# A fused attention and MLP block: DRAM sums sent one per group, a weight combination later in each group, three single window products ahead of the double ones, operand splits in two parts

## The chip, the cores and the metric

The kernel runs on one core of one Trainium2 chip. The metric is the time of one execution in microseconds (us); of several runs the median counts.

## The reference

One input x of 2048 tokens by 576 channels is normalised and goes through two branches, whose sum is the output. Branch A is attention over a dilated window of 8 positions, branch B a token mixer and then an MLP with 4608 hidden channels. All is float32.

```python
def _A_ref(x, wqkv, wo):                      # H = 32 heads of Dh = 18, W = 8, dil = 2
    qkv = (x @ wqkv) -> q, k, v               # by head
    kg, vg = k, v at positions s - 2 * (0..7) # masked before the start
    attn = softmax(einsum("bhsd,bhswd->bhsw", q, kg) * Dh ** -0.5)
    return einsum("bhsw,bhswd->bhsd", attn, vg).reshape(B, S, D) @ wo

def _B_ref(x, w1, w2, w3, w4):
    h = gelu(layernorm(x) @ w1)               # then its quarters shifted by +1, -1, +2, -2 tokens
    x1 = x + shifted(h) @ w2
    return x1 + gelu(layernorm(x1) @ w3) @ w4

xn = layernorm(x)
return x + _A_ref(xn, ...) + _B_ref(xn, ...)
```

## The kernel before

**Numbers and engines.** A float32 value is split into a high part of reduced precision (float32r) and a low part, the rest; a product is made of three matmuls (high by high, high by low, low by high). So each operand is first cast on ScalarE (ACT) and then subtracted on VectorE (DVE). TensorE (PE) does the matmuls, GpSimd (POOL) mainly issues DMAs that add into their destination, SyncE (SP) issues plain DMAs.

**Stages.** After the q, k, v projections, the mixer and the second layer norm, the MLP runs in two stages. In the first, hidden channels are done by `units` u = 0 to 23 (6 pairs of channel blocks by 4 token blocks of 512), with the up product, gelu and down product written out. The second stage does the remaining 24 pairs of hidden blocks and token halves as groups q = 0 to 23; groups 0 to 11 serve the first token half, 12 to 23 the second, with the weights in reverse order. Each of these groups is a 2 by 2 block product done with seven products instead of eight: P1 to P7 multiply sums of weight blocks (tiles `w3a`, with A11, A12, A22, and `w3s`, with S1 to S4) with sums of the activations (B11, B21, B22 from `xn`, and T1 to T4, which are made in DRAM tensors `td` by DMAs that add). Results are gathered in Z1 to Z4 (rows of the tile Y), go through gelu into the hidden tiles `c11`, `c12`, `c21`, `c22`, and D0 to D7 are the down products of the group before, by 128 tokens each. `c12`, `c22` and `c21` have one buffer each, `c11` has two. D0 to D3 read `c12` and `c22`; D4 to D7 read `c11` and `c21`.

**The order.** Nothing schedules the code: each engine carries out its instructions in the order in which they are written. In the second stage a string per group orders PE's work, usually `P1 D0 P2 P6 D1 P5 D2 P7 D3 P4 D4 P3 D5 D6 D7`, in group 11 `P1 D0 P2 P6 P5 P7 D1 P4 P3 D2 D3 D4 D5 D6 D7`, in group 12 `D0 D1 P1 D2 P2 P6 D3 P5 P7 D4 P4 P3 D5 D6 D7`. A `plan` hangs further work behind these steps with `at(step, function)`. The functions that matter:

- `load_pair(q)` (L944, L947) loads the raw W3 blocks into the staging tile `w3st`, which has one buffer; `split_a` casts three of them into `w3a` (ACT L960 and L962, DVE L966) and lets POOL add one 48 KB piece (L963), which reads `w3st`; `combine` (DVE L955, four instructions) then makes the sums in place in `w3st`; `split_s` makes `w3s` from them.
- `sums(sb, step)` (L892 on) builds T1 to T4 of token half sb in DRAM: T1 = n0 top + n1 top, T3 = n1 top + n1 bottom, T2 = n1 bottom + T1, T4 = n0 bottom + T2. Each is one plain DMA from SP and one adding DMA from POOL, 576 KB each.
- `get_op` (L915, L917) loads such an operand, `split_op` (ACT L926 to L928, DVE L595) splits it. In group 11 the operands of the second token half replace those of the first in the same tiles.
- `down` evicts a result: for the ten token tiles in `YD` ACT copies it to a staging tile (L867) and POOL adds it to the DRAM tensor `yd` (L868); for others ACT (L870) or, in the groups around 11 and 12, DVE (L873) adds it in place. Two PSUM banks serve the downs in turn, so Dn needs the eviction of D(n-2). For the in-place tiles ACT first copies the old value into the bank (L843).
- `load_xa(t)` adds the input x to `yd[t]` with a DMA from POOL (L880).
- The attention runs on DVE in the background: after each step `bg` issues some 1.5 us of it, less what the step itself costs DVE (`spent`). For each of 8 groups of four heads the window products are formed in `po` (L740, then a reduction, L743), for one window position (1152 elements per partition) or two at once (2304). `po` has two halves; the first half is also where the output of the head group before is gathered (L716, L720) and stored from to DRAM (`od`, L722). Single products use the second half alone.

## Time and profile before

| what | value |
|---|---|
| median of 3 runs | 1299.88 us (1298.46 to 1302.51) |
| the profiled execution | 1301.5 us |
| its span in the profile | 1299.7 us |
| granted clock of TensorE, mean | 0.994 |
| DMA traffic | 222.66 MB, mean 171 GB/s |

The span runs from the first instruction to the last. An engine's busy time says how much it had to do, not whether it was waited for; the idle time behind "[... <-X]" in a row is what the engine waited in front of that instruction, and X is the instruction or transfer that released it. PEld is the loading of the stationary operand, which runs beside the matmuls; its rows show PE's pauses best. A DMA issued by POOL or SP appears once as an instruction of that engine and once as a transfer, whose "us to landing" counts from its issue.

The groups of the second stage start (P1) at 636.31 us for group 1, then 670.35, 698.24, 725.66, 750.09, 774.15, 798.64, 823.49, 852.61 and 876.95 for groups 2 to 10, 901.01 for group 11, 955.16 for group 13.

### The profile page before, as it was taken

To read this page: it belongs to the slowest core of one execution; us is meant where nothing else is said; L and a number is where in the kernel's file an instruction comes from. 1 tells how busy PE (TensorE), PEld (TensorE's weight loads), DVE (VectorE), ACT (ScalarE), POOL (GpSimd) and SP (SyncE) were. 2 spreads that over 40 slices of the span, in tenths; PEclk is the share of its full clock that TensorE was granted. 3 is DMA by queue.
4 is the path that set the end of the run, shared out by engine and by line. 5 is a ranking of instruction groups with operands and counts; after the bars stand their busy time and mean duration, and the time that the engine had idled before them with its cause. 6 is when DMAs were issued, how large, how long until landed. Compare 5 with 4: busy or idle time off the path is not lost.

```text
span 1299.7 us, 19930 instructions
## 1 busy us (share of the span) xinstructions
PE 1266.1 (97%) x7510; PEld 1158.8 (89%) x7510; DVE 897.3 (69%) x1180; ACT 727.7 (56%) x1162; POOL 252.3 (19%) x366
## 2 busy tenths in 40 slices
PE   8999999999999999999898999899899999999998
PEld 8999998898899998999687998898889999998898
DVE  6456535778568999997556988789788993455342
ACT  3322226526645545556656777667867777667730
POOL 2011100021122212111123232222122222222100
PEclk9999999999999999999999999999999999999999
DMA  7646874246898886769479988868956777899972
GB/s 210 155 112 144 172 165 144 71 141 178 201 264 173 183 170 120 195 125 234 82 200 202 191 154 205 169 156 161 281 104 145 157 134 142 189 219 218 255 249 83
DMA packets 203009, 222.66 MB, mean 171 GB/s; under 512 B 79504, under 2 KB 138736, under 8 KB 202784
## 3 DMA queue, kind: packets, MB, share of 16 engines
q1 hardware_dynamic: 170160, 154.59, 41.4%
q0 software_dynamic: 32752, 66.80, 32.7%
q8 instruction: 59, 0.97, 0.3%
q14 instruction: 38, 0.31, 0.1%
HBM read 122.75 MB, written 107.28 MB: 177 GB/s over the span
## 4 chain that ended last, share of the span: by engine, by line
PE 54%; issue 5%; DMA 5%; ACT 4%; DVE 2%; POOL 1%; SPq 1%; POOLq 0%; DVEq 0%; ACTq 0%
PE ps L862 26%; PE cc L1116 15%; PE p L826 10%; PE ps L214 4%; DMA w3a<-w3st 2%; DMA w3st<-in_B_w_dram 1%; POOL yd L868 1%; DMA x1n<-xn 1%; ACT Y L867 1%; DVE w3st L955 0%; DMA xt<-td1T 0%; ACT c L814 0%; ACT w3s L962 0%; DMA yd<-Y 0%; DVE po L720 0%
## 5 line engine op out<-in xcount | busy, mean ns | idle before, releaser
L862 PEld LDWEIGHTS ps<-w,c 128*128 128x128 f32 x3456 | 478.3, 189 | 36.4 <-ACT Y L867 9.9
L862 PE MATMUL ps<-w,c 128*128 128x288 f32 x3456 | 491.7, 296 | 17.0 <-ACT Y L867 7.6
L868 POOL DMA_DIRECT2D yd<-Y x154 | 140.7, 931 | 450.1 <-ACT Y L867 377.0
L820 DVE TENSOR_TENSOR c<-Y,c 128x512 fp32r<-128x512 f32 x144 | 98.9, 687 | 90.5 <-ACT Y L809 78.8
L867 ACT COPY Y<-ps 128x576 f32<-128x576 f32 x154 | 97.8, 636 | 80.7 <-PE ps L862 66.9
L214 PE MATMUL ps<-WQ,xt 128*128 128x432 f32 x672 | 134.8, 360 | 0.0
L1116 PE MATMUL cc<-xt,w3s 128*128 128x512 f32 (+1 forms) x504 | 129.4, 397 | 3.4 <-DVE Y L1126 3.4
L214 PEld LDWEIGHTS ps<-WQ,xt 128*128 128x128 f32 x672 | 125.6, 188 | 5.7
L1116 PEld LDWEIGHTS cc<-xt,w3s 128*128 128x128 f32 (+1 forms) x504 | 93.2, 190 | 21.7 <-DVE Y L1126 3.6
L1116 PE MATMUL cc<-x1n,w3a 128*128 128x512 f32 (+1 forms) x336 | 87.5, 400 | 3.7 <-ACT cc L1310 1.8
L740 DVE TENSOR_TENSOR po<-q,k 128x2304 f32<-128x2304 f32 (+1 forms) x40 | 83.0, 2075 | 7.7 <-DMA od<-po 7.0
L743 DVE TENSOR_REDUCE L<-po 128x128 f32<-128x2304 f32 (+1 forms) x40 | 82.8, 2071 | 0.6
L121 POOL TENSOR_TENSOR rs<-rs,mhalf 128x1 f32<-128x1 f32 x48 | 30.9, 643 | 260.5 <-DVE rs L120 147.9
L323 ACT COPY stg<-ps 128x864 f32<-128x864 f32 x24 | 21.2, 882 | 102.8 <-PE ps L214 55.8
L955 DVE TENSOR_TENSOR w3st<-w3st 128x384 f32<-128x384 f32 x92 | 51.3, 557 | 37.8 <-DMA w3a<-w3st 18.9
L808 ACT ACTIVATE c<-p 128x512 fp32r<-128x512 f32 x48 | 28.7, 599 | 86.8 <-PE p L826 86.8
L716 DVE TENSOR_TENSOR po<-v,L 128x1152 f32<-128x1152 f32 x56 | 75.6, 1354 | 0.9
L1116 PEld LDWEIGHTS cc<-x1n,w3a 128*128 128x128 f32 (+1 forms) x336 | 61.4, 191 | 16.1 <-ACT cc L1310 2.2
L870 ACT COPY Y<-ps 128x576 f32<-128x576 f32 x92 | 58.9, 640 | 30.0 <-PE ps L862 28.5
L720 DVE TENSOR_TENSOR po<-po 128x1152 f32<-128x1152 f32 x49 | 66.4, 1356 | 1.0
L843 ACT COPY ps<-Y 128x576 f32<-128x576 f32 x92 | 59.4, 645 | 3.5 <-DVE Y L873 1.5
L214 PE MATMUL ps<-W,h 128*128 128x288 f32 x384 | 53.5, 295 | 0.0
(194 smaller groups left out, 1935.9 us busy)
## 6 DMA issues: line engine op xcount, KB each, us to landing
yd<-Y POOLq DMA_DIRECT2D x156, 288.0 KB, 6.2
Y<-in_B_w_dram SPq DMA_DIRECT2D x29, 576.0 KB, 7.5
w3st<-in_B_w_dram SPq DMA_DIRECT2D x56, 256.0 KB, 6.2
qkvd<-stg SPq DMA_DIRECT2D x24, 432.0 KB, 3.5
yd<-ev POOLq DMA_DIRECT2D x26, 288.0 KB, 6.5
w3st<-in_B_w_dram SPq DMA_DIRECT2D x92, 64.0 KB, 6.7
xd<-st SPq DMA_DIRECT2D x16, 320.0 KB, 6.0
xd<-big SPq DMA_DIRECT2D x16, 320.0 KB, 8.5
```

Source lines behind the costliest of these rows:

```text
L214: pe.matmul(ps[:, h, :n], xs(a), ws(b, h), start=i == 0, stop=i == len(PAIRS) - 1)
L716: dve.tensor_tensor(dst, vv, Lf[:, :, w:w + 1].to_broadcast([128, TPP * GH, HD]), op=ALU.mult)
L720: dve.tensor_tensor(o, o, dst, op=ALU.add)
L740: dve.tensor_tensor(dst, qf[:, None, :].to_broadcast([128, n, TPP * GC]), win, op=ALU.mult)
L743: dve.tensor_reduce(Lw[:, w:w + n, :], dst.rearrange("p w (x d) -> p w x d", d=HD), axis=AX.X, op=ALU.add)
L820: dve.tensor_tensor(h[:, 1, :], g, h[:, 0, :].bitcast(F32), op=ALU.subtract)
L826: pe.matmul(ps, W3[f][:, w, :], x1n[b][:, a, :], start=n == 0, stop=n == len(PAIRS) - 1)
L843: act.copy(ps[:, :, :HF], halves(t))
L862: pe.matmul(ps[:, k, :HF], h[:, col], w[:, p, k * HF:(k + 1) * HF], start=n == 0 and not seed, stop=n == len(seq) - 1, skip_group_check=True)
L867: act.copy(e.rearrange("p (h c) -> p h c", h=2), ps[:, :, :HF])
L868: pool.dma_start(yd[t], e, accum_op=ALU.add)
L1116: pe.matmul(ps, WX[w][:k, v, SLOT[w], :], area[sb][xk][:k, a, :], start=onto is None and i == 0, stop=last and i == len(HALVES) - 1, skip_ ...
```

## The change

Five things change.

1. `sums` has eight steps with one DMA each instead of four steps with four, two, one and one. In the first stage they are called in units 4 to 11, in the second behind D6 of groups 1 to 8 (before: behind D2 of groups 1 to 4).
2. `load_xa` of groups 1 to 10 goes from P3 to D7.
3. `combine` goes from D3 to P4, in group 0 from D3 to P3 behind the gelu of Z2, in group 12 from D3 to D4.
4. `split_op` can be called in two parts (two of the three thirds of an operand, then the rest). In groups 11 and 12 the parts are spread over more steps, and the gelus, their low parts and `split_w4` of group 11 go to earlier steps.
5. The window products of the attention are three single ones, two double ones and a single one, instead of two single and three double ones.

```diff
-                for w, n in ((0, 1), (1, 1), (2, 2), (4, 2), (6, 2)):
+                for w, n in ((0, 1), (1, 1), (2, 1), (3, 2), (5, 2), (7, 1)):
...
     def sums(sb, step):
         n0, n1 = xn[2 * sb], xn[2 * sb + 1]
-        if step == 0:
-            sp.dma_start(td[sb, "T1"], n1[0:HF])
-            sp.dma_start(td[sb, "T3"], n1[HF:])
-            sp.dma_start(td[sb, "T2"], n1[HF:])
-            sp.dma_start(td[sb, "T4"], n0[HF:])
-        elif step == 1:
-            pool.dma_start(td[sb, "T1"], n0[0:HF], accum_op=ALU.add, max_dma_last_dim=2048)
-            pool.dma_start(td[sb, "T3"], n1[0:HF], accum_op=ALU.add, max_dma_last_dim=2048)
...
+        k, src, first = (("T1", n1[0:HF], True), ("T1", n0[0:HF], False),
+                         ("T3", n1[HF:], True), ("T3", n1[0:HF], False),
+                         ("T2", n1[HF:], True), ("T2", td[sb, "T1"], False),
+                         ("T4", n0[HF:], True), ("T4", td[sb, "T2"], False))[step]
+        if first:
+            sp.dma_start(td[sb, k], src)
...
+            pool.dma_start(td[sb, k], src, accum_op=ALU.add, max_dma_last_dim=2048)
...
+    def split_op(sb, k, part=None):
...
+        if part != 1:
+            spent[0] += 1.2
+            act.activation(xt[:, 3:5, :], raw[:, 1:3, :], AF.Identity, scale=sg)
+        if part != 0:
+            spent[0] += 0.7
+            rtemps.append(rtemps.pop(0))
+            r = temp(rtemps[-1]).bitcast(F32R)
+            act.activation(r[64:96], raw[64:96, 0, :], AF.Identity, scale=sg)
+            act.activation(xt[0:64, 0, :], raw[0:64, 0, :], AF.Identity, scale=sg)
+        if part != 1:
+            signed(xt[:, 1:3, :], raw[:, 1:3, :], sg, xt[:, 3:5, :])
+        if part != 0:
+            signed(xt[64:96, 0, :], raw[64:96, 0, :], sg, r[64:96])
...
-        if 4 <= u < 12 and u % 2 == 0:
-            sums(0, (u - 4) // 2)
+        if 4 <= u < 12:
+            sums(0, u - 4)
...
-            at("D3", combine, n)
             at("P3", gelu12)
-            at("P3", split_s, n, (0, 1))
+            at("P3", combine, n)
             at("P3", low12)
+            at("P3", split_s, n, (0, 1))
             at("P3", split_s, n, (2,))
...
-            at("D1", split_op, 1, "B11")
-            at("D2", split_op, 1, "B21")
-            at("D3", gelu22)
-            at("D4", low22)
-            at("D4", split_op, 1, "T2")
-            at("D5", gelu12)
-            at("D2", split_w4, p)
-            at("D6", low12)
-            at("D6", split_op, 1, "T1")
-            at("D7", split_op, 1, "T4")
+            at("P4", split_w4, p)
+            at("P4", gelu22)
+            at("P3", split_op, 1, "B11", 0)
+            at("P3", low22)
+            at("D2", split_op, 1, "B11", 1)
+            at("D2", gelu12)
+            at("D3", split_op, 1, "B21", 0)
+            at("D4", low12)
+            at("D4", split_op, 1, "B21", 1)
+            at("D5", split_op, 1, "T2", 0)
+            at("D6", split_op, 1, "T2", 1)
+            at("D7", split_op, 1, "T1", 0)
         elif q == NWP:
...
-            at("D1", split_op, 1, "T3")
+            at("D0", split_op, 1, "T1", 1)
+            at("D1", split_op, 1, "T3", 0)
+            at("P1", split_op, 1, "T3", 1)
+            at("D2", split_op, 1, "T4", 0)
             at("P2", split_a, n, (0, 1))
-            at("D2", split_op, 1, "B22")
             at("P6", split_a, n, (2,))
-            at("D3", combine, n)
+            at("P6", split_op, 1, "T4", 1)
+            at("D3", split_op, 1, "B22", 0)
+            at("P5", split_op, 1, "B22", 1)
+            at("D4", combine, n)
...
-            at("D3", combine, n)
             at("D3", split_w4, p, 0)
+            at("P4", combine, n)
...
-        if 0 < q < 5:
-            at("D2", sums, 1, q - 1)
+        if 0 < q < 9:
+            at("D6", sums, 1, q - 1)
         if 0 < q <= len(YD):
-            at("P3", load_xa, YD[q - 1])
+            at("D7", load_xa, YD[q - 1])
```

Three places show how it moves instructions. The first is POOL, from D1 of group 2 to D1 of group 3. td1T1 and the others are the sums (before L900 and L901, now L901), in_A_x is load_xa (L880), yd1 to yd7 are the evictions, w3a and w3s the small pieces of the W3 splits. Before:

```order
L868 DMA yd5_89<-Y_71 128x576 [waits DMASW3_49,Activation_49]
L963 DMA w3a_6258<-w3st_6170 32x384 [waits DMAHW1_49,DMASW4_49,Activation_49]
L900 DMA td1T1_104<-xn2_98 288x512 [waits DMAHW2_49,DMASW5_49]
L901 DMA td1T3_106<-xn3_99 288x512 [waits DMAHW3_49,DMASW6_49]
L868 DMA yd7_90<-Y_71 128x576 [waits Activation_49]
L963 DMA w3s_6360<-w3st_6170 32x512 [waits DVE_49,DMASW0_49,PE_49,Activation_49]
L880 DMA yd2_87<-in_A_x_dram 128x576 [waits DMASW1_49]
L868 DMA yd1_86<-Y_71 128x576 [waits DMASW2_49,Activation_49]
L868 DMA yd2_87<-Y_71 128x576 [waits DMASW3_49,DMASW1_49,Activation_49]
L868 DMA yd3_88<-Y_71 128x576 [waits DMASW4_49,Activation_49]
L868 DMA yd5_89<-Y_71 128x576 [waits DMASW5_49,Activation_49]
L963 DMA w3a_6497<-w3st_6402 32x384 [waits DMAHW3_49,DMASW6_49,Activation_49]
```

Now:

```order
L868 DMA yd5_89<-Y_71 128x576 [waits DMASW3_49,Activation_49]
L964 DMA w3a_6263<-w3st_6173 32x384 [waits DMAHW5_49,DMASW4_49,Activation_49]
L868 DMA yd7_90<-Y_71 128x576 [waits DMASW5_49,Activation_49]
L964 DMA w3s_6358<-w3st_6173 32x512 [waits DVE_49,DMASW6_49,PE_49,Activation_49]
L868 DMA yd1_86<-Y_71 128x576 [waits DMASW2_49,Activation_49]
L868 DMA yd2_87<-Y_71 128x576 [waits DMASW0_49,Activation_49]
L901 DMA td1T1_104<-xn2_98 288x512 [waits DMAHW0_49,DMASW1_49]
L868 DMA yd3_88<-Y_71 128x576 [waits Activation_49]
L880 DMA yd2_87<-in_A_x_dram 128x576 [waits DMASW3_49,DMASW0_49]
L868 DMA yd5_89<-Y_71 128x576 [waits DMASW4_49,Activation_49]
L964 DMA w3a_6502<-w3st_6398 32x384 [waits DMAHW5_49,DMASW5_49,Activation_49]
```

The pair of sums between the w3a piece and yd7 has become one, behind yd2, and load_xa stands behind the three evictions that end the group. In this group it waits for the eviction into its own tensor, yd2, where before the eviction waited for it.

The second place is ACT in group 11, from D1's eviction (L867) on. c22 is cleared for writing by L814 (gelu22), x1n2 is the operand B11 (and B21), w4 the cast of split_w4. Before:

```order
L867 COPY Y_71<-ps1_8276 128x576 [waits DMASW4_49,PE_49]
L926 ACTIVATE x1n2_5540<-x1n2_5540 128x1024 [waits DMAHW3_49]
L927 ACTIVATE Y_71<-x1n2_5540 32x512 [waits DMAHW6_49]
L928 ACTIVATE x1n2_5540<-x1n2_5540 64x512 [waits DMAHW5_49,DMAHW4_49]
L926 ACTIVATE x1n2_5540<-x1n2_5540 128x1024 [waits DMAHW7_49]
L927 ACTIVATE Y_71<-x1n2_5540 32x512 [waits DMAHW2_49,DVE_49]
L928 ACTIVATE x1n2_5540<-x1n2_5540 64x512 [waits DMAHW1_49,DMAHW0_49]
L567 CAST w4_8292<-Y_71 128x2x576
L867 COPY Y_71<-ps1_8382 128x576 [waits DMASW5_49,PE_49]
L814 ACTIVATE c22_8454<-Y_71 128x512 [waits DVE_49]
```

Now:

```order
L867 COPY Y_71<-ps1_8287 128x576 [waits DMASW3_49,PE_49]
L567 CAST w4_8304<-Y_71 128x2x576 [waits DMAHW2_49]
L814 ACTIVATE c22_8410<-Y_71 128x512 [waits DVE_49,PE_49]
L815 ACTIVATE Y_71<-Y_71 128x512 [waits Activation_49]
L921 ACTIVATE x1n2_5548<-x1n2_5548 128x1024 [waits DMAHW3_49]
L926 ACTIVATE Y_71<-x1n2_5548 32x512 [waits DMAHW6_49]
L927 ACTIVATE x1n2_5548<-x1n2_5548 64x512 [waits DMAHW5_49,DMAHW4_49]
L814 ACTIVATE c12_8445<-Y_71 128x512 [waits DVE_49]
L815 ACTIVATE Y_71<-Y_71 128x512 [waits Activation_49]
L867 COPY Y_71<-ps1_8395 128x576 [waits DMASW4_49]
```

The gelu into c22 stands ahead of B11's cast and of D3's eviction (the last row, ps1_8395), and has a wait for PE of its own, which it did not have behind D3's eviction.

The third place is DVE where one head group of the attention ends and the next but one begins, in group 8. L716 and L720 gather the output, L740 is a window product, L743 its reduction, L955 (now L956) the combination. Before:

```order
L716 TENSOR_TENSOR po<-v,L 128x1152 [waits DVE_49]
L820 TENSOR_TENSOR c_7593<-Y,c_7593 128x512 [waits PE_49,Activation_49]
L720 TENSOR_TENSOR po<-po 128x1152 [waits DVE_49]
L740 TENSOR_TENSOR po<-q,k 128x1152 [waits DMAHW1_49,DVE_49]
L743 TENSOR_REDUCE L<-po 128x64 [waits DVE_49]
L740 TENSOR_TENSOR po<-q,k 128x1152 [waits DVE_49]
L743 TENSOR_REDUCE L<-po 128x64 [waits DVE_49]
L820 TENSOR_TENSOR c_7636<-Y,c_7636 128x512 [waits Activation_49]
L740 TENSOR_TENSOR po<-q,k 128x2304 [waits DMAHW0_49,DVE_49]
L966 TENSOR_TENSOR w3a<-w3st,w3a 128x768 [waits DMAHW2_49,DMAHW1_49,Activation_49]
L1126 TENSOR_TENSOR Y<-cc_7661,Y 128x512 [waits Activation_49]
```

Now:

```order
L720 TENSOR_TENSOR po<-po 128x1152 [waits DVE_49]
L740 TENSOR_TENSOR po<-q,k 128x1152 [waits DMAHW0_49,DVE_49]
L743 TENSOR_REDUCE L<-po 128x64 [waits DVE_49]
L740 TENSOR_TENSOR po<-q,k 128x1152 [waits DVE_49]
L820 TENSOR_TENSOR c_7646<-Y,c_7646 128x512 [waits Activation_49]
L743 TENSOR_REDUCE L<-po 128x64 [waits DVE_49]
L967 TENSOR_TENSOR w3a<-w3st,w3a 128x768 [waits DMAHW1_49,DMAHW0_49,Activation_49]
L1127 TENSOR_TENSOR Y<-cc_7671,Y 128x512 [waits Activation_49]
L740 TENSOR_TENSOR po<-q,k 128x1152 [waits DVE_49]
L743 TENSOR_REDUCE L<-po 128x64 [waits DVE_49]
L956 TENSOR_TENSOR w3st<-w3st 128x3x128 [waits DMAHW3_49,DMAHW4_49,DMAHW2_49,DMAHW5_49,DMASW7_49,DMASW1_49]
```

The double product, which waits for the store of the first half of po (DMAHW0), stood ahead of this group's w3a subtraction and its addition to Z3 (L966, L1126). Now these come first, and there are three single products and the combination before it; it follows at the start of group 9.

14 lines of the change are left out of this document (1 added, 13 removed).

## The prediction

> **What bounds the kernel now.** I read the page's totals first, then the second half of the MLP cut into its groups (from one P1 to the next), then the tensor engine's waits, then the engines named there.
>
> ```profile
> span 1299.7 us, 19930 instructions
> PE 1266.1 (97%) x7510; PEld 1158.8 (89%) x7510; DVE 897.3 (69%) x1180; ACT 727.7 (56%) x1162; POOL 252.3 (19%) x366
> ...
> PE   8999999999999999999898999899899999999998
> ```
>
> PE is busy for 97% of the span, and the change leaves its matmuls as they are. Only the 33.6 us in which PE has nothing to do, and the slower matmuls behind its longer pauses, can be won or added to. The table by groups (length, then busy time of each engine, clock, DMA share, GB/s) tells where they lie:
>
> ```profile
> 636.31:670.35 34.04, 26.75 (x145) 23.18 (x146) 14.61 (x21) 19.22 (x31) 6.69 (x8) 0.95 0.55 143
> 670.35:698.24 27.89, 24.76 (x148) 22.16 (x146) 17.38 (x17) 16.29 (x27) 7.92 (x9) 0.99 0.86 193
> 698.24:725.66 27.42, 25.66 (x147) 23.01 (x147) 22.22 (x27) 19.48 (x30) 9.17 (x11) 0.95 0.90 171
> 725.66:750.09 24.43, 24.33 (x148) 21.84 (x147) 22.69 (x25) 18.49 (x31) 7.93 (x10) 1.00 1.05 228
> 774.15:798.64 24.49, 24.32 (x147) 21.96 (x146) 20.06 (x23) 15.15 (x25) 6.24 (x9) 1.00 0.86 203
> 798.64:823.49 24.85, 24.32 (x147) 21.85 (x146) 23.30 (x25) 21.99 (x34) 7.44 (x10) 1.00 0.69 132
> 823.49:852.61 29.12, 25.74 (x148) 23.02 (x146) 21.63 (x22) 15.38 (x25) 6.87 (x9) 0.94 0.79 172
> 901.01:955.16 54.15, 50.57 (x293) 45.40 (x292) 43.84 (x51) 37.87 (x59) 10.49 (x14) 0.97 0.90 214
> 979.21:1003.28 24.07, 24.07 (x148) 21.95 (x147) 21.49 (x26) 17.12 (x28) 5.94 (x8) 1.00 0.75 170
> ```
>
> The last row is a group that waits for nothing: 24.07 us is the floor. Above it stand group 1 (10.0 us), groups 2 and 3 (3.8 and 3.4), groups 4, 6 and 7 (0.4, 0.4 and 0.8), group 8 (5.1), and the pair 11 and 12 (54.15 less 48.14: 6.0). The pauses themselves, in the order of time (start, busy, what, idle before and its releaser):
>
> ```profile
> 643.24 0.98 PEld L862 LDWEIGHTS ps<-w,c 128*128 128x128 f32 x4 [3.54 <-ACT c L814]
> 644.62 1.94 PEld L862 LDWEIGHTS ps<-w,c 128*128 128x128 f32 x8 [0.41 <-DVE c L820]
> 668.79 1.61 PEld L862 LDWEIGHTS ps<-w,c 128*128 128x128 f32 x12 [2.94 <-ACT Y L867]
> 704.86 1.44 PEld L1116 LDWEIGHTS cc<-x1n,w3a 128*128 128x128 f32 x7 [2.00 <-ACT cc L1310]
> 844.83 2.63 PEld L1116 LDWEIGHTS cc<-xt,w3s 128*128 128x128 f32 x7 [3.61 <-DVE Y L1126]
> 921.81 9.49 PEld L862 LDWEIGHTS ps<-w,c 128*128 128x128 f32 x60 [3.08 <-DVE Y L873]
> ```
>
> PE waits for ACT and DVE, which are not full either. So what do they wait for? The groups of DVE's lines, and its rows at three of these places:
>
> ```profile
> L955 DVE TENSOR_TENSOR w3st<-w3st 128x384 f32<-128x384 f32 x92 | 51.3, 557 | 37.8 <-DMA w3a<-w3st 18.9 <-issue 15.2 <-DVE Y L1126 0.9
> 639.58 2.34 DVE L955 TENSOR_TENSOR w3st<-w3st 128x384 f32<-128x384 f32 x4 [2.33 <-DMA w3a<-w3st]
> 641.84 0.68 DVE L1126 TENSOR_TENSOR Y<-cc,Y 128x512 f32<-128x512 f32 x1
> 643.88 0.69 DVE L820 TENSOR_TENSOR c<-Y,c 128x512 fp32r<-128x512 f32 x1 [1.36 <-ACT Y L815]
> 664.13 2.34 DVE L955 TENSOR_TENSOR w3st<-w3st 128x384 f32<-128x384 f32 x4 [6.30 <-DMA w3a<-w3st]
> 840.75 2.56 DVE L740 TENSOR_TENSOR po<-q,k 128x2304 f32<-128x2304 f32 x1 [5.58 <-DMA od<-po]
> ```
>
> The combination (L955) has to wait until the small accumulating DMA of split_a has read the staging tile it overwrites, and the whole of DVE waits with it. At 840.75 it is the attention that holds DVE: a product of two windows writes both halves of po, and one half is still being stored.
>
> ```profile
> td1T<-xn SPq DMA_DIRECT2D x4, 576.0 KB, 7.6
> w3a<-w3st POOLq DMA_DIRECT2D x1, 48.0 KB, 9.5
> 669.15 1.07 POOL L880 DMA_DIRECT2D yd<-in_A_x_dram  x1
> 675.57 2.68 POOL L868 DMA_DIRECT2D yd<-Y  x3 [5.35 <-ACT ps L843]
> 682.50 0.64 ACT L867 COPY Y<-ps 128x576 f32<-128x576 f32 x1 [4.79 <-DMA yd<-Y]
> 695.10 0.91 POOL L901 DMA_DIRECT2D td1T<-xn  x1 [5.82 <-issue]
> 702.47 0.83 POOL L880 DMA_DIRECT2D yd<-in_A_x_dram  x1 [4.70 <-issue]
> ```
>
> The first two rows are the DMA view of 648 to 672 us: the four sums that SP sends at once, and beside them the w3a transfer of 48 KB that needs 9.5 us. Then POOL stands behind load_xa (its yd[1] is accumulated into right behind it, at D5), issues three evictions late, and ACT waits for a staging tile. In group 2 the second of two accumulating sums holds POOL for 5.82 us, and the next load_xa follows 4.70 late.
>
> **The change part by part.** Sums are made against the profiled execution, 1301.5 us (its span of 1299.7 and 1.8 around it), which is 1.6 above the median of the runs, 1299.88.
>
> *Entry into group 1.* In group 0 the combination goes behind the addition to Z2 and its gelu; only the low part still follows it. Before: combination until 641.92, addition at 641.84, gelu, low part at 643.88. Now the low part can start when the combination ends, 641.92: 1.96 earlier, and D0, whose eight matmuls at 644.62 waited for it, moves with it. **-2.0.**
>
> *Group 1.* The four SP sums beside the w3a transfer become one, a group's end away from it. The transfer took 2.33 after DVE was ready in group 0, with nothing beside it, and there is now one attention step and the next matmul stage in front of the combination. The 6.30 falls below the slack, and with it the 2.94 at 668.79. **-3.0.**
>
> *Groups 2 and 3.* load_xa goes from P3 to D7, behind the evictions of the same group. It can still hold POOL while an eviction into its own tile lands (groups 1 to 3 only), but behind it stand just the next group's D1 and its w3a transfer, five stages away (P1, D0, P2, P6, D1: 8 us by the 24.07 over 15 stages). The pair of POOL sums is broken up. The two groups lost 7.2; I leave 2.0 for the loads of q, k and v, which stay. **-5.2.**
>
> *Group 8.* A third single product comes ahead of the first double one. As the order shows, the double now stands behind the rest of the group, not two singles after the store: three singles with their reductions, the combination (2.34), a low part and the w4 split come between, over 10 us against the 5 or so before, and 5.58 was missing. **-4.8** of the 5.1. The price is two more DVE instructions in each of eight head groups. Two halves against one whole:
>
> ```profile
> L716 DVE TENSOR_TENSOR po<-v,L 128x1152 f32<-128x1152 f32 x56 | 75.6, 1354 | 0.9
> 1065.83 1.35 DVE L720 TENSOR_TENSOR q<-q,po 128x1152 f32<-128x1152 f32 x1
> ```
>
> An instruction over 1152 elements takes 1.354 and one over 2304 took 2.56 (840.75), so a split costs 2.71 less 2.56, 0.15, and sixteen cost 2.4 us of DVE. The attention ends at 1067, and it is only forced to end at P4 of group 18, which begins at 1075.5 (979.21 and four more groups of 24.07); without that cover the 2.4 would stand on the path.
>
> *Groups 4 to 10.* Until now these had no sum after group 4; now groups 1 to 8 have one each, sent at D6 with load_pair, whose landing the first step of the next split_a needs by D1. The median landing of load_pair's large pieces was, in the views of 648 to 672 and of 822 to 846:
>
> ```profile
> w3st<-in_B_w_dram SPq DMA_DIRECT2D x2, 256.0 KB, 3.2
> w3st<-in_B_w_dram SPq DMA_DIRECT2D x2, 256.0 KB, 9.3
> ```
>
> 3.2 alone and 9.3 in a crowd, so a sum beside it can cost between nothing and 6.1 of landing; D6 to D1 leaves about 8 to 10. Below nothing is possible too, since the load_xa leaves the stage before. Bounds for the seven groups: they lose the 1.6 they have now less all of it, or as much as group 3 lost with its sum (3.4) in every second one (13). I take **+1.5**, near the low end, since group 4 ran with a sum at a DMA share of 1.05 and lost only 0.4.
>
> *Groups 11 and 12.* Here the splits are cut in two and the gelu of Z3 (gelu22) goes from D3 to P4. But in group 11 P4 comes before D2 and D3, and both still read c22 of the group before, of which there is one buffer. ACT therefore stops at gelu22 until D3 is done, and D4 follows D3 directly. Between them now lie, one after the other: two gelus, the cast of B11, its subtraction on DVE, the low part of c22, and D2's eviction on DVE, which frees D4's bank. Rows of the same instructions:
>
> ```profile
> 914.80 1.06 ACT L926 ACTIVATE x1n<-x1n 128x1024 fp32r<-128x1024 f32 x1 [1.55 <-DMA x1n<-xn]
> 921.15 0.63 ACT L814 ACTIVATE c<-Y 128x512 fp32r<-128x512 f32 x1
> 921.81 0.63 ACT L815 ACTIVATE Y<-Y 128x512 f32<-128x512 f32 x1
> 921.00 0.75 DVE L873 TENSOR_TENSOR Y<-ps,Y 128x576 f32<-128x576 f32 x1
> 921.67 1.22 DVE L595 SCALAR_TENSOR_TENSOR x1n<-x1n 128x1024 fp32r<-128x1024 f32 x1
> ```
>
> 0.63 + 0.63 + 1.06 + 1.22 + 0.69 + 0.75 is 5.0, against the 3.08 that D4 waits today for B11's late landing (914.80). ACT is also busy almost without a break from there on, so a late start is carried along. From 0 (the parts fill gaps of ACT) to +5 (nothing is made up), I take **+2.0**.
>
> The stall of 5.0 is followed by slow matmuls: 2.63 for seven weight loads at 844.83, behind 3.61 idle, 1.44 at 704.86 behind 2.00. The Trainium skill ("TensorE: Matmul & The Clock Gate", Part 1) says that the clock halves after an idle window of about 3.4 us; the trace agrees in so far as 2.94 at 668.79 left full speed behind. By that rule the transition would cost some 1 to 1.5 more, which lies within the +5.
>
> The first half's sums, now one a unit in units 4 to 11, I take at nothing: slices 13 to 18 of PE's row on the page (390 to 585 us), which hold them, stand at nine tenths or more, and the up products there do not wait for them.
>
> Sum: -2.0 - 3.0 - 5.2 - 4.8 + 1.5 + 2.0 = -11.5. 1301.5 - 11.5 = 1290.0 as a profiled execution, less 1.6: **1288.4** for the median.
>
> **The rivals.**
> *Crowding moves to D6.* Load_pair, the sum, three evictions, load_xa and the w4 load now stand within ten us. For it: 9.3 for a load_pair in a crowd. Against it: group 4's 24.43. Each of groups 1 to 8 would lose about 1.2 (a third of the mean of group 2's and 3's loss, 3.6): +9.6 instead of +1.5, 1296.5. The Trainium skill ("DMA: Bandwidth & Descriptors", Queues, rings and completion order) has each DMA engine take turns between queues, packet by packet, which speaks for this one: a sum from POOL would take half the engines' turns from load_pair. No run here shows the turns one by one.
> *Slower: POOL is held at D7.* One mechanism: load_xa at D7 waits for an eviction to land or for room behind a sum, and holds the next w3a transfer; then the combination stops DVE in each of ten groups. The point is a wait on POOL over about 8 us (5.82 is the longest so far). Price: the 8.2 of groups 1 to 3 are not won, and 1.3 in ten groups is lost (a third of the 3.8 in group 2): 1288.4 + 8.2 + 13 = 1309.6.
> *The transition breaks.* ACT, 5 us late at gelu22, never catches up, and T1, T3, T4 and B22 each come late: +8 instead of +2, 1294.4.
> *The double product's order does nothing*, since the store starts elsewhere in a group: 1293.2.
>
> **How the numbers follow.** Forecast 0.58, crowding 0.17, POOL held 0.08, broken transition 0.09, double product 0.08. A measurement here tells 0.3% from nothing, that is 1296.0 to 1303.8. Faster: 0.58 + 0.09 + 0.08 = 0.75. Same: most of crowding, 0.16. Slower: 0.09. The forecast's own bounds are 1281.3 (groups 2 and 3 without the 2.0 left to them, groups 4 to 10 at -1.6 instead of +1.5, +0 in the transition) to 1294.0 (+5 in the transition, half of the 5.2 in groups 2 and 3). Reaching into crowding gives 1281 to 1299.
>
> **What would show it.** Right: no DVE wait over 2 us at the combination in groups 1 to 3; groups 1 to 4 and 8 under 25 us apart from group 1's entry; no wait of ACT for yd; a PE pause of about 5 us ahead of D4 in group 11, with ACT idle at gelu22. Wrong: DVE still waits for w3a, or new pauses at D1 to P4 behind a late load_pair in groups 5 to 8.

## The result, and the profile after

| kernel | median, us | of runs | lowest to highest |
|---|---|---|---|
| before | 1299.22 | 12 | 1297.83 to 1303.91 |
| changed | 1304.09 | 12 | 1301.96 to 1307.86 |

The ratio is 1.0037, 95% interval 1.0024 to 1.0050: slower by 0.4%, where 1288.4 and a gain were forecast. The profiled execution took 1304.09 us.

The page's first lines: the same matmuls, sixteen more DVE instructions, as expected, and a longer span.

```profile
span 1302.3 us, 19944 instructions
PE 1267.3 (97%) x7510; PEld 1162.0 (89%) x7510; DVE 900.6 (69%) x1196; ACT 728.4 (56%) x1162; POOL 252.4 (19%) x366
```

To compare kernels group by group I use the copy of `cc` on ACT, which follows P1 once in every group from 1 on; from one copy to the next lie 24.06 us where nothing waits. The table by stretches, groups 1 to 10 and then 11 and 12 together (length, then busy time of each engine, clock, DMA share, GB/s):

```profile
640.97:665.27 24.30, 24.30 (x141) 22.03 (x140) 10.53 (x14) 16.87 (x29) 6.45 (x8) 0.96 0.53 102
665.27:689.33 24.06, 24.06 (x147) 21.94 (x146) 21.46 (x21) 17.19 (x28) 6.28 (x8) 1.00 0.77 162
689.33:718.42 29.09, 26.13 (x147) 23.16 (x146) 22.99 (x25) 20.16 (x30) 8.73 (x10) 0.94 0.83 197
718.42:742.49 24.07, 24.07 (x147) 21.95 (x146) 20.82 (x22) 17.00 (x28) 5.94 (x7) 1.00 0.97 226
742.49:773.36 30.87, 26.79 (x147) 24.17 (x146) 23.63 (x21) 17.05 (x27) 9.50 (x11) 0.89 0.74 135
773.36:797.83 24.47, 24.32 (x147) 21.96 (x146) 19.58 (x25) 17.00 (x28) 5.23 (x7) 1.00 0.81 211
797.83:825.49 27.66, 25.85 (x147) 23.45 (x146) 22.57 (x23) 20.13 (x30) 8.73 (x11) 0.94 0.77 148
825.49:849.55 24.06, 24.06 (x147) 21.93 (x146) 21.94 (x22) 17.18 (x27) 5.99 (x8) 1.00 0.93 227
849.55:875.25 25.70, 24.31 (x147) 21.96 (x146) 19.88 (x19) 16.99 (x27) 7.88 (x9) 1.00 0.80 147
875.25:901.76 26.51, 24.59 (x147) 22.00 (x146) 22.57 (x27) 19.50 (x29) 7.26 (x9) 1.00 0.77 185
901.76:958.41 56.65, 50.31 (x292) 45.47 (x291) 43.81 (x50) 38.03 (x59) 10.88 (x14) 0.97 0.86 205
```

Groups 1, 2 and 8, which had lost most before, now lose next to nothing. In their place groups 3, 5, 7 and 9 lose: exactly the groups behind a group whose sum is one of POOL's. (Group 10 loses 2.5 as well; experiment 5 shows where that comes from.) What happens in group 3, on POOL (the sum of group 2 at D6, D7's eviction, load_xa at D7, then the evictions of the next group and its w3a transfer):

```profile
690.14 0.94 POOL L901 DMA_DIRECT2D td1T<-xn  x1 [1.83 <-issue]
693.26 0.89 POOL L868 DMA_DIRECT2D yd<-Y  x1 [2.18 <-ACT ps L843]
700.94 0.83 POOL L880 DMA_DIRECT2D yd<-in_A_x_dram  x1 [6.79 <-issue]
701.78 0.90 POOL L868 DMA_DIRECT2D yd<-Y  x1
702.33 1.15 POOL L964 DMA_DIRECT2D w3a<-w3st  x1
```

and on ACT, DVE and PE, in the same order of events:

```profile
697.84 0.62 ACT L963 ACTIVATE w3a<-w3st,kv 96x384 fp32r<-96x384 f32 x1
...
708.70 2.34 DVE L956 TENSOR_TENSOR w3st<-w3st 128x384 f32<-128x384 f32 x4 [3.72 <-DMA yd<-Y]
...
711.11 1.04 ACT L961 CAST w3s<-w3st 128x1024 fp32r<-128x1024 f32 x1 [1.83 <-issue]
...
713.36 1.72 PEld L862 LDWEIGHTS ps<-w,c 128*128 128x128 f32 x12 [2.42 <-ACT Y L867]
```

The first transfer behind the sum goes out 3.1 us after it, the second only 10.8 us after it (in groups 4, 6 and 8 the first after 2.8 to 3.3, the second after 9.6, 10.3 and 9.3). ACT had the w3a piece ready at 698.46 (697.84 and 0.62), and its transfer is issued at 702.33, 3.9 late. By the DMA view of 688 to 706 us it takes 6.3 us, so it lands at 708.6. DVE stands 3.72 at the combination, which starts at 708.70 (the row names the transfer of an eviction issued beside w3a), ACT's cast of w3s waits for it, the eviction L867 stands behind that cast, and PE waits for the bank. The combination's row over the whole kernel, with all that DVE waited there:

```profile
L956 DVE TENSOR_TENSOR w3st<-w3st 128x384 f32<-128x384 f32 x92 | 51.3, 558 | 36.7 <-issue 23.5 <-DMA yd<-Y 3.7 <-DMA xd<-big 2.6
```

36.7 us against 37.8 before: the wait that the change was to remove has only moved.

### The profile page after: what moved, and what is told of

Same layout as the page of the kernel before. It is cut to its first block, busy times and chain, and to the rows that moved or that the text cites. A ratio compares the mean times of both kernels' runs of the same rounds, so it can differ in the third digit from the quotient of the medians.

```text
span 1302.3 us, 19944 instructions
## 1 busy us (share of the span) xinstructions
PE 1267.3 (97%) x7510; PEld 1162.0 (89%) x7510; DVE 900.6 (69%) x1196; ACT 728.4 (56%) x1162; POOL 252.4 (19%) x366
## 5 line engine op out<-in xcount | busy, mean ns | idle before, releaser
L862 PE MATMUL ps<-w,c 128*128 128x288 f32 x3456 | 494.4, 297 | 25.9 <-ACT Y L867 11.9
L867 ACT COPY Y<-ps 128x576 f32<-128x576 f32 x154 | 97.6, 634 | 76.2 <-PE ps L862 71.2
L740 DVE TENSOR_TENSOR po<-q,k 128x1152 f32<-128x1152 f32 (+1 forms) x48 | 84.2, 1754 | 0.8
L743 DVE TENSOR_REDUCE L<-po 128x64 f32<-128x1152 f32 (+1 forms) x48 | 84.0, 1751 | 0.8
L956 DVE TENSOR_TENSOR w3st<-w3st 128x384 f32<-128x384 f32 x92 | 51.3, 558 | 36.7 <-issue 23.5
L716 DVE TENSOR_TENSOR po<-v,L 128x1152 f32<-128x1152 f32 x56 | 75.2, 1354 | 0.9
L720 DVE TENSOR_TENSOR po<-po 128x1152 f32<-128x1152 f32 x49 | 66.4, 1355 | 1.0
```

Of the source, the lines that this page charges most:

```text
L716: dve.tensor_tensor(dst, vv, Lf[:, :, w:w + 1].to_broadcast([128, TPP * GH, HD]), op=ALU.mult)
L720: dve.tensor_tensor(o, o, dst, op=ALU.add)
L740: dve.tensor_tensor(dst, qf[:, None, :].to_broadcast([128, n, TPP * GC]), win, op=ALU.mult)
L743: dve.tensor_reduce(Lw[:, w:w + n, :], dst.rearrange("p w (x d) -> p w x d", d=HD), axis=AX.X, op=ALU.add)
L862: pe.matmul(ps[:, k, :HF], h[:, col], w[:, p, k * HF:(k + 1) * HF], start=n == 0 and not seed, stop=n == len(seq) - 1, skip_group_check=True)
L867: act.copy(e.rearrange("p (h c) -> p h c", h=2), ps[:, :, :HF])
```

## The experiments

Sixteen kernels ran, each against the kernel before on the same chip. In the table, beside median and ratio, what the profile shows: the start of the first copy of `cc` (entry), and what each group lost over 24.06, worked out from the starts of that copy in each kernel's trace. From group 13's copy to the end, a part that most of these edits leave alone, single profiles differ by up to 3.7 us (341.1 to 344.8), so a row of this table is read group by group, and the medians tell what an edit is worth. The kernel before ran again with each set of experiments (medians 1299.22 to 1300.90), so a difference between two kernels can come out up to 1.5 us otherwise by the ratios than by the medians, which the text uses where it does not say ratios.

| kernel | median | ratio, 95% interval | entry | groups 1 to 10 | 11+12 |
|---|---|---|---|---|---|
| before | | | 645.32 | 2.9 7.9 -0.2 -0.1 0 1.3 -0.1 5.5 -0.1 0 | 6.0 |
| changed | 1304.09 | 1.0037 (1.0024 to 1.0050) | 640.97 | 0.2 0 5.0 0 6.8 0.4 3.6 0 1.6 2.5 | 8.5 |
| 1 changed, load_xa at P3 | 1303.29 | 1.0022 (1.0013 to 1.0031) | 643.55 | -0.7 3.6 4.6 0 4.8 0.5 2.6 0 0.2 2.4 | 9.1 |
| 2 changed, sums at D2 | 1293.55 | 0.9948 (0.9933 to 0.9964) | 642.70 | 1.4 0 1.9 2.1 0 0.4 0 0 0 2.3 | 9.3 |
| 3 changed, combination at D3 | 1307.17 | 1.0056 (1.0041 to 1.0071) | 641.09 | 0.3 0 3.5 0 6.3 0.5 5.4 0 3.5 2.2 | 9.5 |
| 4 changed, old plans of 11, 12 | 1303.14 | 1.0026 (1.0011 to 1.0040) | 642.17 | 0.1 0 3.2 0 6.4 0.5 4.7 0 6.3 0 | 5.6 |
| 5 before, third single product | 1296.73 | 0.9976 (0.9964 to 0.9988) | 645.20 | 3.4 3.9 4.7 0 0 0.5 0 0 0 1.6 | 6.1 |
| 6 before, sums singly at D6 | 1305.78 | 1.0044 (1.0021 to 1.0066) | 645.49 | 0 2.5 2.5 -0.1 3.8 1.3 4.2 5.2 2.2 -0.1 | 5.8 |
| 7 before, sums singly at D2 | 1291.95 | 0.9938 (0.9922 to 0.9955) | 644.98 | 1.0 2.6 -0.1 0 0 1.6 -0.1 4.6 -0.1 0 | 5.8 |
| 8 changed, POOL's sums in 8 KB rows | 1302.94 | 1.0017 (0.9995 to 1.0039) | 641.10 | 0.2 0 7.1 0 5.4 0.6 0.2 0.4 6.2 3.5 | 8.8 |
| 9 changed, POOL's sums at D2, SP's at D6 | 1293.68 | 0.9957 (0.9942 to 0.9972) | 643.63 | 0.8 0 2.2 2.8 0 0.5 0 0 1.4 1.7 | 9.5 |
| 10 two parts: 5 and 7 | 1286.95 | 0.9903 (0.9886 to 0.9920) | 644.15 | 0.3 0 1.7 0 0 0.4 0 0 0 1.6 | 5.1 |
| 11 three parts: 10, combination later | 1285.86 | 0.9891 (0.9874 to 0.9908) | 640.97 | 1.6 0 1.7 0 0 0.2 0 0 0 1.3 | 5.3 |
| 12 as 11, load_xa at D7 | 1293.84 | 0.9952 (0.9938 to 0.9967) | 642.42 | 0.9 0 2.4 2.3 0 0.6 0 0 0 2.1 | 7.7 |
| 13 as 11, D7 in groups 1 to 3 | 1288.66 | 0.9907 (0.9888 to 0.9925) | 643.13 | 0.9 0 2.0 2.8 0 0.4 0 0.2 0 1.9 | 6.0 |
| 14 as 11, D7 in groups 4 to 10 | 1288.65 | 0.9905 (0.9884 to 0.9926) | 643.36 | 0.8 0.2 2.0 0 0 0.6 0 0.1 0 1.8 | 7.9 |
| 15 as 11, load_xa in groups 13 to 22 | 1284.34 | 0.9867 (0.9843 to 0.9891) | 642.91 | 0.5 0 0.9 0 0 0.1 0 0 0 0 | 4.5 |
| 16 as 11, POOL's sums in 8 KB rows | 1285.50 | 0.9889 (0.9866 to 0.9911) | 643.70 | 0.9 1.1 2.3 0 0 0.5 0 0 0 1.1 | 6.5 |

**1. load_xa back at P3.**

```diff
-            at("D7", load_xa, YD[q - 1])
+            at("P3", load_xa, YD[q - 1])
```

> The changed kernel with load_xa back at P3; the sums stay at D6, one per group. Theory (POOL is held): with nothing of POOL's behind the sum at D6 but D7's eviction, the waits of 5.6 to 6.8 us on POOL before load_xa (L880) go, the combine of groups 3, 5, 7 and 9 no longer waits 3.7 to 4.3, and the time falls by 4 to 7 us to 1297 to 1300. Rival (crowding: the sum slows load_pair and the w3a transfer on the DMA engines, and POOL's order does not matter): the combine still waits over 3 us in those groups and the time stays within 2 us of 1304.

The gain is 0.8 us (2.0 by the ratios, whose intervals overlap): the theory missed in this form, and the rival's number came. POOL around the sum of group 2, and the combination behind it:

```profile
697.59 0.94 POOL L901 DMA_DIRECT2D td1T<-xn  x1 [0.28 <-issue]
703.54 0.89 POOL L868 DMA_DIRECT2D yd<-Y  x1 [5.01 <-ACT w3a L961]
709.18 0.85 POOL L868 DMA_DIRECT2D yd<-Y  x1 [4.75 <-issue]
709.73 1.12 POOL L964 DMA_DIRECT2D w3a<-w3st  x1
```

```profile
715.08 2.34 DVE L956 TENSOR_TENSOR w3st<-w3st 128x384 f32<-128x384 f32 x4 [4.80 <-DMA w3a<-w3st]
```

Without load_xa it is the next eviction that is held, here until 11.6 us after the sum (9.8, 9.4 and 8.5 in groups 4, 6 and 8), and the w3a transfer stands behind it. Which transfer is held makes little difference; in both kernels w3a stands behind the held one.

**2. The sums at D2.**

```diff
-            at("D6", sums, 1, q - 1)
+            at("D2", sums, 1, q - 1)
```

> The changed kernel with its eight sums at D2, right behind the group's w3a transfer; load_xa stays at D7. Theory (POOL is held): the sum's room is free again by D7, some 10 us later, load_xa waits for no room, and the time falls to 1297 to 1301; what remains is evictions held behind the sum at D3 and D4 in groups 2, 4, 6 and 8. Rival (load_xa at D7 alone is enough, by the wait for an eviction of its own tile): waits over 5 us at L880 stay in most groups and the time stays at 1302 to 1306.

10.5 us less than the changed kernel, more than expected. Groups 3, 5, 7 and 9 lose 1.9 in all, in group 3 alone, in place of 17.1. POOL in group 2 and at its end:

```profile
677.47 0.77 POOL L964 DMA_DIRECT2D w3a<-w3st  x1 [1.00 <-ACT w3a L963]
678.14 1.07 POOL L901 DMA_DIRECT2D td1T<-xn  x1
682.01 0.90 POOL L868 DMA_DIRECT2D yd<-Y  x1 [2.80 <-ACT Y L867]
687.82 0.77 POOL L964 DMA_DIRECT2D w3s<-w3st  x1 [4.92 <-ACT w3s L963]
...
696.51 0.84 POOL L880 DMA_DIRECT2D yd<-in_A_x_dram  x1 [4.05 <-DMA yd<-Y]
```

The sum now follows the w3a transfer. The second transfer behind it is w3s, 9.7 us later, when ACT has it ready anyway: the hold is covered.

**3. The combination back at D3.**

```diff
+            at("D3", combine, n)
             at("D3", split_w4, p, 0)
-            at("P4", combine, n)
```

> The changed kernel with the combine of the general groups back at D3. Rival theory (the later combine uses up its own slack, so that the w3s pieces come too late): the time falls by 3 to 5 us to 1299 to 1301. Theory (POOL is held): the w3a transfer comes as late as before, the combine stands 2 to 3 us sooner in front of it, waits 6 to 7 instead of about 4 in groups 3, 5, 7 and 9, and DVE's evictions of D3 and D4 wait with it: 1306 to 1310.

3.1 more (2.5 by the ratios, whose intervals just overlap), and DVE's waits at the combination in groups 3, 5, 7 and 9 were 5.15, 7.31, 6.66 and 5.89. The later combination is not what costs; if anything it makes up for a part.

**4. The old plans of groups 11 and 12.**

The diff of the change in these two branches, undone.

> The changed kernel with the plans of groups 11 and 12 as they were (whole splits, gelu of Z3 at D3 in group 11). Theory: the new plan costs what the two groups lost more, 8.5 against 6.0: the PE pause ahead of D4 in group 11 falls from 5.2 to about 3, and the time falls by 2 to 3 us to 1301 to 1302. Rival (what is lost there is carried in from group 10, late w3s and ACT): no change, 1303 to 1305.

1.0 less, within the spread of the runs: neither number is told apart. The profile does show the two groups at 5.6 in place of 8.5, but in this execution group 9 lost 6.3 in place of 1.6.

**5. The third single product alone.**

```diff
-                for w, n in ((0, 1), (1, 1), (2, 2), (4, 2), (6, 2)):
+                for w, n in ((0, 1), (1, 1), (2, 1), (3, 2), (5, 2), (7, 1)):
```

> The kernel before with the third single product alone. Theory (the step of the prediction on group 8 is right): DVE's wait of 5.58 at the first double product goes, group 8 falls from 29.1 to 24.5 or so, and the time falls by 4 to 5 us to 1294.5 to 1296. Rival (the stall was carried in from elsewhere, or the two more DVE instructions a group cost on the path): 1299 to 1301.

3.6 less, a little under the 4 to 5 forecast. Group 8's 5.5 is gone, as the prediction had it (and in this profile group 2 loses 4.0 less). But groups 3 and 10 now lose 4.7 and 1.6, where the kernel before loses next to nothing. The edit also delays the loads of q and k: SP issues them at 703.53 and 704.00 us, ahead of a w4 load in its queue (706.42), where in the kernel before they went out behind one (679.68 and 680.08, behind 676.05). The w4 load of 576 KB, which `split_w4` casts, then takes 11.9 us to land in group 3 and 9.5 in group 10, in place of 8.5 and 8.1. ACT waits for it 3.37 and 2.19, and PE waits for ACT. PE in group 3 and ACT in group 10:

```profile
722.64 4.74 PEld L862 LDWEIGHTS ps<-w,c 128*128 128x128 f32 x24 [2.20 <-ACT Y L870]
```

```profile
889.76 1.16 ACT L567 CAST w<-Y 128x1152 fp32r<-128x1152 f32 x1 [2.19 <-DMA Y<-in_B_w_dram]
```

In the traces of all fifteen kernels with the third single product ACT waits for w4 in group 3 (1.3 to 6.0 us), in fourteen of them in group 10 too (0.2 to 3.2); in the three without it, it waits in neither. So the changed kernel's 2.5 in group 10, and the 1.9 that group 3 still loses in experiment 2, go with this part of the change and not with the sums.

**6 and 7. The sums alone, singly at D6 and singly at D2.** Both have the change's `sums`, called in units 4 to 11. The call of 6 is below; 7 has D2 in place of D6.

```diff
-        if 0 < q < 5:
-            at("D2", sums, 1, q - 1)
+        if 0 < q < 9:
+            at("D6", sums, 1, q - 1)
```

> The kernel before with the sums alone changed as in the change: one transfer per group, at D6 of groups 1 to 8 (load_xa at P3 and the combine at D3 as before). Theory (a sum from POOL holds the second transfer behind it for some 10 us, and from D6 that reaches over the next w3a transfer, in four groups): the combine at D3 waits 5 to 7 us in groups 3, 5, 7 and 9, groups 1 and 2 gain 4 or so, and the time rises by 4 to 10 us to 1303 to 1309. Rival (one transfer per group is cheap wherever it stands): 1293 to 1299.

> The kernel before with its sums one per group at D2 of groups 1 to 8, and nothing else. Theory: right behind the w3a transfer a sum has some 8 us until the w3s transfer needs POOL, so what is held is evictions alone; the burst of four SP sums in group 1 and the pair in group 2 are broken up, and the time falls by 3 to 7 us to 1293 to 1297. Rival (the eight transfers cost as much wherever they stand, and the gain with D2 came from the other parts): 1299 to 1302.

5.5 more at D6, 8.4 less at D2: the place of one call decides nearly 14 us, with everything else as before. At D6 groups 1 and 2 gain 8.3 together and groups 3, 5, 7 and 9 lose 13.1 more.

**8. The same bytes in fewer, longer rows.**

```diff
-            pool.dma_start(td[sb, k], src, accum_op=ALU.add, max_dma_last_dim=2048)
+            fold = lambda a: a.rearrange("(r b) c -> r (b c)", b=4)
+            pool.dma_start(fold(td[sb, k]), fold(src), accum_op=ALU.add,
+                           max_dma_last_dim=8192)
```

> The changed kernel with each sum from POOL sent as 72 rows of 8 KB in place of 288 rows of 2 KB: the same bytes. Theory 1 (POOL is held for lack of room for outstanding rows, so a quarter of the rows needs a quarter of the room): the waits of 5.6 to 6.8 at L880 fall below 2, the combine in groups 3, 5, 7 and 9 no longer waits, and the time falls to 1293 to 1298. Theory 2 (POOL is held until the sum's bytes have landed, some 10 us whatever the rows): the waits stay, 1302 to 1306.

Each theory is half right. The hold is shorter: the second transfer behind a sum goes out 5.3, 6.0, 6.3 and 4.5 us after it, in place of 10.8, 9.6, 10.3 and 9.3, while the sum itself still takes 9 to 10 us to land. So POOL is not held until the sum has landed; what it waits for grows with the number of rows, as room for outstanding rows would. But the median hardly moves (1.2 less, 2.6 by the ratios). The twelve runs lie between 1295.6 and 1309.5, far wider than those of the changed kernel, and the profiled one, 1305.8, is among the slower; what follows is read from it. The DMA view of 684 to 702 us (queue or transfer, count, KB each, median us to landing) shows what takes the gain back. The changed kernel, then this one:

```profile
td1T<-xn POOLq DMA_DIRECT2D x1, 576.0 KB, 10.5
q<-qkvd SPq DMA_DIRECT2D x1, 576.0 KB, 7.2
k<-qkvd SPq DMA_DIRECT2D x1, 576.0 KB, 9.6
Y<-in_B_w_dram SPq DMA_DIRECT2D x1, 576.0 KB, 10.5
...
w3st<-in_B_w_dram SPq DMA_DIRECT2D x4, 64.0 KB, 5.6
```

```profile
td1T<-xn POOLq DMA_DIRECT2D x1, 576.0 KB, 9.0
q<-qkvd SPq DMA_DIRECT2D x1, 576.0 KB, 10.8
k<-qkvd SPq DMA_DIRECT2D x1, 576.0 KB, 13.2
Y<-in_B_w_dram SPq DMA_DIRECT2D x1, 576.0 KB, 14.6
...
w3st<-in_B_w_dram SPq DMA_DIRECT2D x4, 64.0 KB, 8.4
```

The sum lands 1.5 sooner and SP's transfers beside it 2.8 to 4.1 later, the pieces of load_pair among them, which ACT needs for the next w3a. Behind the other three sums it is alike: the 64 KB pieces land after 9.8, 9.2 and 12.4 in place of 5.7, 6.0 and 5.8, the w4 loads after 12.0, 11.5 and 12.7 in place of 9.1, 9.5 and 7.8. In group 5 of this kernel ACT waits for the pieces, and the w3a transfer is late again:

```profile
755.53 0.62 ACT L965 ACTIVATE w3a<-w3st,kv 96x384 fp32r<-96x384 f32 x1 [3.04 <-DMA w3st<-in_B_w_dram]
```

In group 9 it waits 7.02 for load_pair, and in group 3, where w3a is in time (the combination waits 0.87), 5.95 for the w4 load. So in this profile the crowding stands behind the hold. The Trainium skill ("DMA: Bandwidth & Descriptors", Queues, rings and completion order) says that a DMA engine goes round its queues packet by packet; that longer rows in POOL's queue slow SP's transfers agrees with it (7.2 to 10.8 for q), though no run shows the turns one by one.

**9. Only POOL's sums moved to D2.**

```diff
+            at("D2" if q % 2 == 0 else "D6", sums, 1, q - 1)
```

> The changed kernel with POOL's four sums at D2 and SP's four at D6, all of one size. Theory (what costs at D6 is above all that a sum from POOL holds POOL's queue): nothing of POOL's is held at D7, the time is that of all eight at D2, 1292 to 1295. Rival (crowding: any sum of 576 KB at D6 makes load_pair land late for the next D1): half of the gain of D2 is lost again, 1297 to 1300, with ACT waiting at the second piece of the w3a split (L963) for w3st in groups 2, 4, 6 and 8.

As good as all eight at D2. SP's sums at D6 cost nothing that can be measured; they are issued behind load_pair in the same queue and do not pass through POOL's. The loss at D6 is that of POOL's four sums.

**10 to 12. Building it up again.** 10 is the kernel before with the edits of 5 and 7; 11 adds the later combination of groups 0 to 10; 12 adds load_xa at D7.

> The kernel before with two parts only: the third single product, and the sums one per group at D2. Alone they gave 3.6 and 8.4 less. Theory (they end different pauses: groups 8 and 1 to 3): they add, 1286 to 1290. Rival (the stall that one removes is taken up by the other's, as ACT and POOL are late together): 1291 to 1293.

> As the kernel with two parts, and the combine later (groups 0 to 10 as in the change); load_xa stays at P3, the plans of groups 11 and 12 as before. Theory (entry into group 1 gains 2.0, elsewhere the later combine does no harm when the w3a transfer is in time): 2 less than the kernel with two parts, 1284 to 1288. Rival (the later combine makes the w3s pieces late in every group): the same or 1 to 3 more than the kernel with two parts.

> As the kernel with three parts, and load_xa at D7: the whole change but for the plans of groups 11 and 12, with the sums at D2. Against all of it with the sums at D2 (1293.6) it gives the price of the new plans of 11 and 12: 0 to 3 less, 1290.5 to 1293.5, if they cost what the two profiles say (8.5 against 6.0 lost there). Against the kernel with three parts it gives load_xa's place: theory (at D7 it is held by the eviction into its own tile in groups 1 to 3 and holds POOL ahead of the w3a transfer): 2 to 5 more than with three parts; rival (its place does not matter once the sums are gone from D6): within 1.

The two parts add (3.6 and 8.4 alone, 12.9 together). The later combination gives 1.1 by the medians, which their spreads do not tell from the 2 expected. load_xa at D7 takes 8.0 back, in a kernel with no sum at D6; and 12 against 2 (1293.84 and 1293.55) gives the new plans of 11 and 12 no price. The profiles do give them one: the six kernels with the new plans lose 8.5 to 9.5 in groups 11 and 12, the twelve with the old ones 4.5 to 7.9. Where the medians take it back stays open.

**13 to 15. Where load_xa costs.** Edits of the line in experiment 1: D7 where q < 4 and P3 elsewhere; the reverse; and P3 of groups 13 to 22.

> The kernel with three parts (1285.9), with load_xa at D7 in groups 1 to 3 alone. Theory 1 (it waits 2.3, 4.8 and 7.3 us there for evictions into its own tile and holds POOL ahead of the w3a transfer): most of the 8 us, 1290 to 1294. Theory 2 (it crowds load_pair in each of ten groups): three tenths of it, 1287 to 1289.

> The kernel with three parts, with load_xa at D7 in groups 4 to 10 alone. Theory 1 (the wait for evictions of its own tile): nothing of the 8 us, 1285 to 1287. Theory 2 (crowding in each group): seven tenths, 1290 to 1293.

> The kernel with three parts, with load_xa at P3 of groups 13 to 22 in place of 1 to 10. If load_xa at P3 still costs the first groups something (its transfer beside the evictions that wait for its tile): 2 to 5 less, 1281 to 1284. If P3 is as good as none: 1285 to 1287; if groups 13 to 22 have no room on POOL either: over 1288.

By the ratios against 11 the halves cost 2.1 and 1.8 us, less than the 3 or so by which two such ratios must differ to be told apart, so the times alone prove a cost for neither half and decide between the theories in neither case. The profiles show a loss for each, at different places. In groups 1 to 3 it is the wait for the tile's own eviction, longest in group 3, whose D7 evicts that tile just ahead; POOL and DVE of 13:

```profile
727.23 0.85 POOL L880 DMA_DIRECT2D yd<-in_A_x_dram  x1 [8.23 <-DMA yd<-Y]
727.82 1.17 POOL L868 DMA_DIRECT2D yd<-Y  x1
728.38 1.41 POOL L959 DMA_DIRECT2D w3a<-w3st  x1
```

```profile
735.04 2.33 DVE L951 TENSOR_TENSOR w3st<-w3st 128x384 f32<-128x384 f32 x4 [3.03 <-DMA w3a<-w3st]
```

and group 4 loses 2.8. It loses 2.1 to 2.8 in each of the four kernels with load_xa at D7 of groups 1 to 3 and no POOL sum at D6 (2, 9, 12 and 13), and nothing in the six that have neither (7, 10, 11, 14, 15 and 16). In groups 4 to 10 the loss stands in groups 11 and 12 (7.9 against 5.3); by what path was not tried. In groups 1 to 12 the profiles of 13 and 14 lose 4.1 and 3.3 more than 11, that of 12 loses 5.9 more; by the ratios it is 2.1, 1.8 and 7.9, each to within some 3 us. Whether the halves add to the whole stays open. With load_xa out of these groups altogether (15) group 10 loses nothing more (ACT waits 0.23 for w4 there in place of 1.93) and 11 and 12 lose 4.5. It is the fastest kernel here, 1.3% under before (0.9867), though its interval overlaps that of 11.

**16. Longer rows at D2.**

> The kernel with three parts, with each of POOL's sums as 72 rows of 8 KB. At D2 the hold behind a sum falls on evictions alone. If these still cost: 1 to 3 less, 1283 to 1285. If the hold is wholly covered at D2: 1285 to 1287.

The same as 11 by the median (its runs lie wider, 1282.8 to 1291.5). At D2 nothing is to be won by shortening the hold.

## Why the prediction was wrong

Its terms against the two profiles, by the copies of `cc`:

| term | predicted | measured | how |
|---|---|---|---|
| entry into group 1 | -2.0 | -4.4 | 645.32 to 640.97; -2.6 as a mean of 13 kernels with the later combination against 5 without |
| group 1 | -3.0 | -2.7 | 2.9 to 0.2 |
| groups 2 and 3 | -5.2 | -2.7 | group 2 7.9 to 0, but group 3 -0.2 to 5.0 |
| group 8 | -4.8 | -5.5 | 5.5 to 0 |
| groups 4 to 10 without 8 | +1.5 | +13.9 | 1.0 to 14.9 |
| groups 11 and 12 | +2.0 | +2.5 | 6.0 to 8.5 |
| behind group 12 | 0 | +1.3 | not touched by the change |

Before rounding they add to +2.6, the difference of the two spans. Cut at the copies, the 3.8 and 3.4 that the prediction's cut at P1 gave groups 2 and 3 stand in group 2 alone (7.9 and -0.2).

**Right** were the entry, groups 1, 2 and 8, and the mechanism of the transition, where the pause came as described, 5.16 against the 5.0 that the sum of rows gave:

```profile
922.68 11.09 PEld L862 LDWEIGHTS ps<-w,c 128*128 128x128 f32 x72 [5.16 <-issue]
```

What the new plans cost in time stays open (experiments 4 and 12). The price of the two more DVE instructions was right in kind: DVE's busy time rose by 3.3 (2.4 forecast), and experiment 5 gains with it. That the third single product would also put q and k ahead of w4 in SP's queue, with losses in groups 3 and 10, was not in the prediction.

The prediction added slow matmuls behind a long pause to the transition alone. They came elsewhere too. Twelve weight loads take 1.61 us at a granted clock of 1.00 (709.33 in the changed kernel); in groups 5 and 7 they took

```profile
767.38 2.90 PEld L862 LDWEIGHTS ps<-w,c 128*128 128x128 f32 x12 [4.32 <-ACT Y L867]
820.44 2.76 PEld L862 LDWEIGHTS ps<-w,c 128*128 128x128 f32 x12 [2.04 <-ACT Y L867]
```

with a granted clock of 0.50 (768 to 771 us) and 0.61 (820 to 823), where 2.94 in the kernel before (668.79) was followed by the usual 1.61. So the length of a pause alone does not tell what follows it, and of the 6.8 lost in group 5 4.3 are the pause itself. Of the prediction's two examples only the first is slow: 1.44 for seven loads at 704.86 is usual, since seven such loads take 1.48 with no pause ahead (673.56 in the kernel before).

**The step that failed** is the place of POOL's sums, and it stands in the text twice. For groups 2 and 3 it said that behind load_xa at D7 there is only "the next group's D1 and its w3a transfer, five stages away", 8 us. That counts the slack from load_xa. The hold counts from the sum one step earlier and lasts 9 to 11, so the slack was gone before w3a came up. The 5.82 and 4.70 that the trace of before showed behind a sum were read as what a hold costs wherever it falls. The 5.82 is that of a second sum directly behind the first (issued at 688.34 and 695.10, 6.8 apart); the 4.70 is what was left, when load_xa arrived, of a hold that had begun 7.4 us earlier with the second sum.

For groups 4 to 10 it then took +1.5, "near the low end, since group 4 ran with a sum at a DMA share of 1.05 and lost only 0.4". That sum stood at D2, behind the w3a transfer, and the row says nothing of a sum at D6 ahead of the next. The upper bound, "as much as group 3 lost with its sum (3.4) in every second one (13)", was close (3.4 in three groups is 10.2, in four 13.6), and groups 5, 7 and 9 lose 12.0 of the 14.9. The 2.5 of group 10 goes with w4 (experiment 5).

Of the rivals, "POOL is held at D7" named the right engine and the right chain (1309.6 forecast, 1304.1 measured), but gave it load_xa as its cause and "a wait on POOL over about 8 us" as its point. Waits of 5.6 to 6.8 were enough, and without load_xa there (experiment 1) the time was nearly the same, 0.8 less. "Crowding moves to D6" was there too, hidden behind the hold: it appears when the hold is shortened (experiment 8), and sums from SP, in load_pair's own queue, show none of it (experiment 9).

**load_xa at D7** was taken to be harmless but for groups 1 to 3, with 2.0 left for groups 2 and 3. With the sums at D6 it costs 0.8; with them out of the way 8.0 (12 against 11). The two moves share one loss, which is why undoing either alone tells little of it: undoing the sums gives 10.5, undoing load_xa 0.8, undoing both 18 (11 against the changed kernel; their other difference, the plans of 11 and 12, is not told from nothing).

## What to carry to other kernels

When a DMA is moved in a queue that waits for room, count from the large transfer to the second transfer behind it, and ask which urgent one stands there; put the large one right behind the urgent one, not ahead of it. A wait in a trace is only the part of a hold that was not covered; its length is counted from the instruction that began it. Price a moved instruction by a row at its new place, and where no row has that place, take the bound seriously: here one call at D6 or at D2 made a difference of nearly 14 us. And when an edit on one engine shifts a load, look at what now stands behind that load in its queue, as w4 did behind q and k.
